# Longer store rows, smaller column slabs and one merged weight load at the end of an attention and soft-MoE kernel

## The chip, the cores and the metric

The kernel runs on one core of one Trainium2 chip. The metric is device time in microseconds (us), median of several executions.

Five engines work side by side: TensorE (PE in the profile, PEld for its weight loads), VectorE (DVE), ScalarE (ACT), GpSimd (POOL) and SyncE (SP). Sixteen DMA engines move data between the main memory (HBM) and the on-chip memory. In this kernel GpSimd issues nearly all loads, because they cast fp32 to bf16 on the way, and SyncE issues the stores (and two early loads). The profile shows the two kinds as queue q0 (software_dynamic) and q1 (hardware_dynamic).

## The reference, cut to what matters

```python
# q, k, v: (8 batches, 8 heads, 576, 64) fp32; windowed attention, first 4 heads plain, last 4 dilated
attn_out = _attn_ref(q, k, v)
x = attn_out.transpose(0, 2, 1, 3).reshape(4608, 512)      # tokens x model width
logits = x @ phi                                            # (4608, 32): 8 experts x 4 slots
d = softmax(logits, axis=0)                                 # over the tokens
slot_input = (d.T @ x).reshape(8, 4, 512)
for e in range(8):                                          # w1: (8, 512, 1024), w2: (8, 1024, 512)
    slot_out[e] = np.maximum(slot_input[e] @ w1[e], 0.0) @ w2[e]
c = softmax(logits, axis=1)                                 # over the slots
return c @ slot_out                                         # (4608, 512) fp32
```

No output token can be made before the last token has been read (softmax over the tokens) and all experts are through, so the 9.4 MB of output can only be stored at the end. The reads are 61.9 MB, 33.6 MB of them expert weights.

## The kernel before

A small scheduler places operations on the engines in an order worked out when the kernel is built, and adds the semaphore waits. The attention runs first; the weights stream in between and behind its inputs on the same queue. The end of the kernel is arranged so that loads and stores join: the second weights of the last experts (w2) are loaded in column slabs. The slab of the first 256 output columns comes first, its results are finished and stored for some tokens, and meanwhile the slab of the other 256 columns arrives. The loads in question:

```python
wq += [w1_piece(e, 2 if e == 0 else 0) for e in range(8)]
wq += [w2_piece(e) for e in range(5)] + [w2_piece(5, 0, 4), w2_piece(5, 4, 4)]   # full rows: 16 KB each in HBM, 8 KB for the halves of 5
for s in range(2):                                                               # two column slabs: rows of 1 KB in HBM
    wq += [w2_slab(6, s), w2_slab(7, s, 0, 4), w2_slab(7, s, 4, 2),
           w2_slab(7, s, 6, 1), w2_slab(7, s, 7, 1)]
```

The second expert layer: columns 0 to 511 at once for experts 0 to 5, then by slab (x = 1, 2) for 6 and 7; an add joins the two parts:

```python
l2((0, 1, 2, 3), 0, 0, 512)
l2((4,), 0, 0, 512)
for y in range(2):
    l2((5,), 0, 0, 512, range(4 * y, 4 * y + 4), [b_w5h[y]])
# ... SOx, SOy: the sums of experts 0 to 5 leave PSUM
for x in (1, 2):
    l2((6,), x, 256 * x - 256, 256, bufs=[b_w2[6][x - 1]])
    for y, cs in enumerate((range(4), range(4, 6), range(6, 7), range(7, 8))):
        l2((7,), x, 256 * x - 256, 256, cs, [b_w2h[y][x - 1]])
    op(DVE, lambda x=x: dve.tensor_tensor( ... AluOp.add) ... name=f"SO{x - 1}")
```

The output: nine groups of 512 tokens, four tiles of 128 tokens in each. A tile is one matmul, then an eviction (scaled copy) on ScalarE or VectorE in turn. The first two and a half groups are stored by column halves (ten stores of 256 KB, rows of 1 KB), half a group as one of 512 KB, the other six in full (stores of 1 MB, rows of 8 KB):

```python
for G, x in halves:                        # 2.5 groups, columns 0 to 255
    for j in (x, x + 1):
        out_tile(G, j, 0, 256, ...)
    store(G, 0, 256, ..., x, 2)
# ... the same for columns 256 to 511
for G, x in [(2, 2)] + [(G, x) for G in range(3, 9) for x in (0, 2)]:
    for j in (x, x + 1):
        out_tile(G, j, 0, 512, T2 + 10 + G + .1 * x)
    if G < NA:
        store(G, 0, 512, T2 + 10 + G + .1 * x + .1, x, 2)
    elif x:
        store(G, 0, 512, T2 + 10 + G + .3)
```

The softmax here doesn't subtract the row's maximum and nothing guards it: scores larger than these inputs give would overflow.

## Time and profile before

| | before |
|---|---|
| time, median (lowest to highest) | 177.54 us (177.39 to 177.60), 3 runs |
| span of the profiled run | 175.6 us |
| busy share: TensorE, VectorE, ScalarE | 73%, 68%, 60% |
| HBM read and written | 61.9 and 9.4 MB, 406 GB/s over the span |
| last weight bytes arrive | 151.38 us |
| first store bytes flow | 149.45 us |
| last store bytes flow | 174.81 us |

The last three rows are from the packet records of the trace. The lines of the profile that carry the reading stand in the prediction below. In the lists of stretches the last two columns are the mean busy share of the 16 DMA engines and the GB/s that they moved. A share can exceed 1, since packets overlap. Loads are counted by the bytes that they write, which is half of what they read.

### The profile page before, as it was taken

The numbers are of one execution on the slowest core, as the hardware profiler recorded it, in microseconds if no ns is written. First come the engines' busy times: TensorE is split into PE (matmuls) and PEld (weight loads), VectorE is DVE, ScalarE is ACT, GpSimd is POOL, SyncE is SP. The second block draws the span as 40 slices with busy tenths as digits, with TensorE's granted clock in tenths as the row PEclk, the third lists the DMA queues.
The fourth block names the chain that finished last, engine by engine and source line by source line (L and its number), as shares of the span: only waits on it lengthen the run. The fifth ranks groups of instructions, "written<-read, shape, count | busy, mean of one in ns | idle before, by whom it ended". The sixth has DMA issues, their size and how long they took to land.

```text
span 175.6 us, 4785 instructions
## 1 busy us (share of the span) xinstructions
PE 128.6 (73%) x2102; PEld 87.1 (50%) x2102; DVE 120.2 (68%) x218; ACT 105.2 (60%) x165; POOL 44.8 (25%) x90
## 2 busy tenths in 40 slices
PE   0008767977999999999998988999576748897000
PEld 0005545665777776766767756777343324531000
DVE  6899387968899898998998898349230013499200
ACT  2404664677988988988969959965603013299000
POOL 7659503402523232207500004950000000000000
PEclk9999995589999999999999999999999996999855
DMA  6999999999999999999999999999999999999997
GB/s 187 233 210 215 210 216 210 223 205 210 222 208 213 225 202 215 217 209 214 216 214 211 216 216 216 215 216 216 218 213 205 207 195 188 301 317 414 424 424 313
DMA packets 15700, 41.26 MB, mean 235 GB/s; under 512 B 1728, under 2 KB 8384, under 8 KB 13248
## 3 DMA queue, kind: packets, MB, share of 16 engines
q0 software_dynamic: 11536, 30.41, 88.9%
q1 hardware_dynamic: 4144, 10.55, 15.8%
q8 instruction: 16, 0.26, 0.5%
q14 instruction: 4, 0.03, 0.0%
HBM read 61.93 MB, written 9.44 MB: 406 GB/s over the span
## 4 chain that ended last, share of the span: by engine, by line
DMA 31%; PE 25%; DVE 22%; ACT 7%; POOL 5%; issue 2%; POOLq 0%; DVEq 0%
DMA ar<-in_moe_w_dram 20%; DMA ar<-in_v_dram 11%; PE ps L527 7%; DVE ar L932 6%; ACT ar L566 5%; DVE ar L495 5%; PE ps L588 3%; POOL ar L379 3%; PE ps L534 2%; PE ps L711 2%; DVE ar L501 2%; DVE ar L632 2%; PE ps L544 2%; PE ps L621 2%; DVE ar L452 2%
## 5 line engine op out<-in xcount | busy, mean ns | idle before, releaser
L566 ACT ACTIVATE ar<-ps 128x1152 bf16<-128x1152 f32 (+1 forms) x32 | 37.9, 1185 | 22.7 <-PE ps L551 11.6
L527 PE MATMUL ps<-ar 128*128 128x320 bf16 (+1 forms) x128 | 23.9, 313 | 16.2 <-DVE ar L501 13.8
L495 DVE STREAM_TRANSPOSE ar<-ar 128x576 uint32<-128x576 uint32 x28 | 32.9, 1233 | 0.5 <-DMA ar<-in_v_dram 0.5
L632 DVE TENSOR_TENSOR ar<-ps,fs 96x768 bf16<-96x768 f32 (+1 forms) x32 | 26.3, 823 | 1.1
L594 ACT ACTIVATE ar<-ps 128x768 bf16<-128x768 bf16 x32 | 24.8, 810 | 2.8 <-PE ps L588 2.3
L527 PEld LDWEIGHTS ps<-ar 128*128 128x128 bf16 x128 | 10.9, 102 | 21.5 <-POOL ar L425 13.7
L621 PE MATMUL ps<-ar 128*128 128x65 bf16 x320 | 15.4, 196 | 3.6 <-ACT ar L566 2.0
L588 PE MATMUL ps<-ar 128*128 128x128 bf16 x192 | 16.2, 233 | 0.5 <-DVE ar L632 0.2
L929 ACT ACTIVATE ar<-ps,fs 128x512 f32<-128x512 f32 (+1 forms) x23 | 11.5, 635 | 8.2 <-PE ps L920 8.2
L621 PEld LDWEIGHTS ps<-ar 128*128 128x128 bf16 x320 | 12.3, 98 | 6.8 <-ACT ar L566 2.9
L343 POOL DMA_DIRECT2D ar<-in_k_dram x14 | 7.5, 541 | 31.8 <-DVE ar L495 16.2
L628 DVE RECIPROCAL fs<-ps 96x12 f32<-96x12 f32 (+1 forms) x32 | 6.5, 204 | 12.7 <-PE ps L621 12.4
L501 DVE STREAM_TRANSPOSE ar<-ar 128x576 uint32<-128x576 uint32 x12 | 14.6, 1241 | 0.0
L588 PEld LDWEIGHTS ps<-ar 128*128 128x128 bf16 x192 | 13.1, 120 | 1.9 <-DVE ar L656 1.0
L932 DVE TENSOR_SCALAR ar<-ps,fs 128x512 f32<-128x512 f32 (+1 forms) x23 | 12.7, 626 | 1.2 <-PE ps L920 1.2
L876 PE MATMUL ps<-ar 128*32 128x512 bf16 (+1 forms) x80 | 10.4, 348 | 4.2 <-DMA ar<-in_moe_w_dram 3.5
L920 PE MATMUL ps<-ar 128*128 128x512 bf16 (+1 forms) x46 | 10.6, 360 | 1.3 <-DVE ar L900 1.0
L711 PE MATMUL ps<-ar 128*128 128x288 bf16 x64 | 10.2, 307 | 1.2 <-ACT ar L695 1.2
L341 POOL DMA_DIRECT2D ar<-in_q_dram x16 | 8.8, 548 | 6.1 <-DVE ar L507 6.1
L688 ACT ACTIVATE ar<-ps 128x576 bf16<-128x576 bf16 x16 | 9.5, 648 | 1.2 <-PE ps L672 0.8
L691 ACT ACTIVATE ar<-ps 128x1024 bf16<-128x1024 bf16 x8 | 8.2, 1030 | 2.9 <-PE ps L678 2.9
L507 DVE STREAM_TRANSPOSE ar<-ar 128x160 uint32<-128x160 uint32 (+1 forms) x32 | 9.6, 413 | 0.0
(78 smaller groups left out, 189.6 us busy)
## 6 DMA issues: line engine op xcount, KB each, us to landing
ar<-in_moe_w_dram POOLq DMA_DIRECT2D x12, 1024.0 KB, 25.0
out_dram<-ar SPq DMA_DIRECT2D x6, 1024.0 KB, 8.6
ar<-in_k_dram POOLq DMA_DIRECT2D x16, 288.0 KB, 13.5
ar<-in_q_dram POOLq DMA_DIRECT2D x16, 288.0 KB, 15.6
ar<-in_v_dram POOLq DMA_DIRECT2D x16, 288.0 KB, 14.3
ar<-in_moe_w_dram POOLq DMA_DIRECT2D x5, 512.0 KB, 31.7
out_dram<-ar SPq DMA_DIRECT2D x10, 256.0 KB, 3.5
ar<-in_moe_w_dram SPq DMA_DIRECT2D x1, 1024.0 KB, 5.0
```

The source lines that it names most:

```text
L495: return dve.transpose(au(o_kqv[kq] + 2304 * j + 36 * x, [[1, 18], [36, 16], [576, 2]]), au(src + 64 * 18 * x, [[32, 18], [1, 32]]))
L501: return dve.transpose(au(dst, [[1, 18], [18, 32]]), au(src, [[32, 18], [1, 32]]))
L527: pe.matmul(pf(h, 0, [[1, W]]), a(o_id, [[1, 128]]), a(msk, [[1, W]]), start=True, stop=False)
L566: eo = op(ACT, lambda P=P, W=W: act.activation(a(P, [[W, 4], [1, W]]), AP(ps, 0, [[4096, 128], [512, 4], [1, W]]), ACTF.Exp, scale=SCALE), ...
L588: last = pe.transpose(pb(bank.idx, bb * 256 + par * 32, [[64, 4], [1, 32]]), src, a(o_id, [[1, 128]]))
L594: op(ACT, lambda t=t, bank=bank: act.activation(a(o_vb[vs] + 3 * t * VBK, [[66, 12], [2, 32], [1, 2]]), pb(bank.idx, 0, [[64, 12], [1, 32] ...
L621: last = pe.matmul(pf(bank.idx + x, 65 * t, [[1, 65]]), w, a(VB + t * VBK + 66 * h, [[1, 65]]), start=True, stop=True)
L632: op(DVE, lambda hp=hp, bank=bank: dve.tensor_tensor(a(ox + 128 * hp, [[64, 2], [256, NT], [1, 64]], 0, rows), pf(bank.idx, 0, [[512, 2], ...
L711: last = pe.matmul(pf(bank.idx, 0, [[1, 288]]), a(o_phis + 128 * c, [[1, 128]]), a(o_xt[xt] + 576 * c + 288 * g, [[1, 288]]), start=(c == ...
L920: op(PE, lambda: pe.matmul(pf(bank.idx, 0, [[1, cw]]), a(o_et + 512 * G + j, [[4, 128]]), a(o_so + c0, [[1, cw]]), start=True, stop=True), ...
L929: op(ACT, lambda: act.activation(dst, src(), ACTF.Copy, scale=sca), actt(cw, .1), prio + .1, reads=[bank, b_rinv], writes=wr, name=f"OE{G} ...
L932: op(DVE, lambda: dve.tensor_scalar(dst, src(), sca, None, op0=AluOp.mult), dvet(cw, True) + .08, prio + .1, reads=[bank, b_rinv], writes= ...
```

## The change

Three things. The column slabs become smaller: the first half of expert 6's hidden rows is loaded in full rows, so the two column slabs together hold 3 MB instead of 4. Expert 5 comes in one transfer. And the last 2048 tokens become two groups of eight tiles, each stored in one transfer of 2 MB with rows of 16 KB. The row sums (the denominators of the second softmax) must be grouped like the output, so they are cut anew. Intent: loads with longer rows, stores with longer rows, and first stores that do not dry up before the second columns are ready. Core of the diff:

```diff
+RS_AT = {13: ((0, 3), (3, 1), (4, 1))}
+RSP = 16
@@
-        if i in (9, 13):
-            row_sums(0 if i == 9 else 3, 3 if i == 9 else 6, 15 * PERIOD)
+        if i in RS_AT:
+            for g, n in RS_AT[i]:
+                row_sums(g, n, RSP * PERIOD + 16)
@@
-    wq += [w2_piece(e) for e in range(5)] + [w2_piece(5, 0, 4), w2_piece(5, 4, 4)]
+    wq += [w2_piece(e) for e in range(6)] + [w2_piece(6, 0, 4)]
     for s in range(2):
-        wq += [w2_slab(6, s), w2_slab(7, s, 0, 4), w2_slab(7, s, 4, 2),
+        wq += [w2_slab(6, s, 4, 4), w2_slab(7, s, 0, 4), w2_slab(7, s, 4, 2),
                w2_slab(7, s, 6, 1), w2_slab(7, s, 7, 1)]
@@
+    GROUPS = [(0, 4), (512, 4), (1024, 4), (1536, 8), (2560, 8), (3584, 8)]
@@
-    for y in range(2):
-        l2((5,), 0, 0, 512, range(4 * y, 4 * y + 4), [b_w5h[y]])
+    l2((5,), 0, 0, 512)
+    l2((6,), 0, 0, 512, range(4), [b_w6h])
@@
-        l2((6,), x, 256 * x - 256, 256, bufs=[b_w2[6][x - 1]])
+        l2((6,), x, 256 * x - 256, 256, range(4, 8), [b_w2[6][x - 1]])
@@
-        op(PE, lambda: pe.matmul(pf(bank.idx, 0, [[1, cw]]), a(o_et + 512 * G + j, [[4, 128]]),
+        op(PE, lambda: pe.matmul(pf(bank.idx, 0, [[1, cw]]), a(o_et + t0 + j, [[n, 128]]),
@@
-    for G, x in [(2, 2)] + [(G, x) for G in range(3, 9) for x in (0, 2)]:
...
+    for G, js in [(2, (2, 3))] + [(G, range(8)) for G in range(3, 6)]:
+        for j in js:
+            out_tile(G, j, 0, 512, T2 + 10 + G + .1 * j)
+            if j == js[-1] or G == 3 and j == 3:
+                n = 4 if G == 3 else len(js)
+                store(G, 0, 512, T2 + 10 + G + .1 * j + .05, j + 1 - n, n)
```

This is an excerpt; cuts are marked by @@ and dots. The first group of eight is still stored in two halves of 1 MB.

More of the change, by code (lines that the diff above doesn't have):

```diff
@@ L310, in bass_dilated_sliding_attn__then__soft_moe_slots_kernel @@
     b_sx = Buf("sx")
-    b_w5h = [Buf(f"w5h{x}") for x in range(2)]
+    b_w6h = Buf("w6h")
     b_w2h = [[Buf(f"w2h{x}{s}") for s in range(2)] for x in range(4)]
@@ L374, in fn @@
                 moe_w2[e].rearrange("(p c) f -> p (c f)", c=8)[:, c0 * DM:(c0 + n) * DM])
-        return (fn, n << 18, f"w2_{e}{c0}", b_w2[e] if e < 5 else [b_w5h[c0 // 4]])
+        return (fn, n << 18, f"w2_{e}{c0}", b_w2[e] if e < 6 else [b_w6h])
     def w2_slab(e, s, c0=0, n=8):
@@ L381, in fn @@
                 moe_w2[e].rearrange("(p c) f -> p c f", c=8)[:, c0:c0 + n, 256 * s:256 * s + 256])
-        return (fn, n << 17, f"w2s_{e}{s}{c0}", [b_w2[e][s] if n == 8 else b_w2h[(0, 4, 6, 7).index(c0)][s]])
+        return (fn, n << 17, f"w2s_{e}{s}{c0}", [b_w2[e][s] if e == 6 else b_w2h[(0, 4, 6, 7).index(c0)][s]])
     wq += [w1_piece(e, 2 if e == 0 else 0) for e in range(8)]
-    wq += [w2_piece(e) for e in range(5)] + [w2_piece(5, 0, 4), w2_piece(5, 4, 4)]
+    wq += [w2_piece(e) for e in range(6)] + [w2_piece(6, 0, 4)]
     for s in range(2):
-        wq += [w2_slab(6, s), w2_slab(7, s, 0, 4), w2_slab(7, s, 4, 2),
+        wq += [w2_slab(6, s, 4, 4), w2_slab(7, s, 0, 4), w2_slab(7, s, 4, 2),
                w2_slab(7, s, 6, 1), w2_slab(7, s, 7, 1)]
@@ L765, in half, with rcol, row_sums @@
            rmw=[b_sid] if b < 7 else [], writes=[b_sdb] if b == 7 else [], name=f"SD{b}")
-    def row_sums(g0, g1, prio):
-        n = (g1 - g0) // 3
-        bank = Bank(f"rs{g0}", n)
+    GROUPS = [(0, 4), (512, 4), (1024, 4), (1536, 8), (2560, 8), (3584, 8)]
+    def rcol(G):
+        return o_rinv + GROUPS[G][0] // 128
+    def row_sums(g0, n, prio):
+        t0, nj = GROUPS[g0]
+        w = 32 * nj * n
+        bank = Bank(f"rs{g0}")
         def fn():
             last = None
-            for m in range(n):
-                for qd in range(4):
-                    last = pe.matmul(pf(bank.idx + m, 0, [[1, 384]], 32 * qd, 32), a(o_rm, [[1, 32]]),
-                                     a(o_et + 512 * (g0 + 3 * m) + 128 * qd, [[512, 3], [1, 4], [4, 32]]),
-                                     start=True, stop=True)
-            return last
-        op(PE, fn, pet(4 * n, 384), prio, reads=[b_et, b_rm], writes=[bank], name=f"RS{g0}")
-        op(DVE, lambda: dve.transpose(af(o_rt, [[384, n], [1, 384]]), pf(bank.idx, 0, [[512, n], [1, 384]])),
-           .1 + .4 * n, prio + .1, reads=[bank], writes=[b_rt], name=f"RT{g0}")
-        op(DVE, lambda: dve.reciprocal(f(o_rinv + 4 * g0, [[1, 12 * n]]), af(o_rt, [[32, 12 * n]])),
+            for qd in range(4):
+                last = pe.matmul(pf(bank.idx, 0, [[1, w]], 32 * qd, 32), a(o_rm, [[1, 32]]),
+                                 a(o_et + t0 + 32 * nj * qd, [[128 * nj, n], [1, nj], [nj, 32]]),
+                                 start=True, stop=True)
+            return last
+        op(PE, fn, pet(4, w), prio, reads=[b_et, b_rm], writes=[bank], name=f"RS{g0}")
+        op(DVE, lambda: dve.transpose(af(o_rt, [[1, w]]), pf(bank.idx, 0, [[1, w]])),
+           .1 + w / 960, prio + .1, reads=[bank], writes=[b_rt], name=f"RT{g0}")
+        op(DVE, lambda: dve.reciprocal(f(rcol(g0), [[1, w // 32]]), af(o_rt, [[32, w // 32]])),
            .2, prio + .2, reads=[b_rt], writes=[b_rinv], name=f"RR{g0}")
@@ L828, in bass_dilated_sliding_attn__then__soft_moe_slots_kernel @@
        reads=[bank], writes=[b_sit], name="sid")
-    row_sums(6, 9, T1 + 4)
+    row_sums(5, 1, T1 + 4)
     for x in range(2):
@@ L878, in fn @@
                                      a(w2off(e) + DM * c + col, [[1, n]]),
-                                     start=(c == 0 and (g == 0 or x > 0)),
-                                     stop=(c == 7 and (x > 0 or e in (2, 3, 4, 5))))
+                                     start=(c == 0 and g == 0 or x > 0 and c == (4 if e == 6 else 0)),
+                                     stop=(c == (3 if e == 6 and x == 0 else 7) and (x > 0 or e in (3, 4, 5, 6))))
             return last
@@ L907, in bass_dilated_sliding_attn__then__soft_moe_slots_kernel, with over @@
     NA = 2.5
-    b_og = [[[Buf(f"og{G}{j}{s}") for s in range(2)] for j in range(4)] for G in range(9)]
+    b_og = [[[Buf(f"og{G}{j}{s}") for s in range(2)] for j in range(n)] for G, (_, n) in enumerate(GROUPS)]
     store_ops = []
-    l1_bufs = b_w1 + [x for y in b_w2[:1] for x in y]
     ne = [0]
     def ostg(G):
-        return o_w1 + 4096 * G if G < 8 else o_w2
+        return o_w1 + 8 * GROUPS[G][0]
+    def over(G):
+        t0, n = GROUPS[G]
+        e = range(t0 // 512, t0 // 512 + n // 4)
+        return [x for y in e for x in ([b_w1[y]] if y < 8 else b_w2[0])]
     def out_tile(G, j, c0, cw, prio):
         bank = Bank(f"o{G}{j}{c0}")
-        t = 4 * G + j
+        t0, n = GROUPS[G]
         rd = [b_so[s] for s in range(2) if c0 < 256 * (s + 1) and c0 + cw > 256 * s]
-        op(PE, lambda: pe.matmul(pf(bank.idx, 0, [[1, cw]]), a(o_et + 512 * G + j, [[4, 128]]),
+        op(PE, lambda: pe.matmul(pf(bank.idx, 0, [[1, cw]]), a(o_et + t0 + j, [[n, 128]]),
                                  a(o_so + c0, [[1, cw]]), start=True, stop=True),
@@ L924, in out_tile @@
         src = lambda: pf(bank.idx, 0, [[1, cw]])
-        wr = [b_og[G][j][s] for s in range(2) if c0 < 256 * (s + 1) and c0 + cw > 256 * s]
-        wr = wr + ([b_w1[G]] if G < 8 else b_w2[0])
-        sca = f(o_rinv + t, [[1, 1]])
+        wr = [b_og[G][j][s] for s in range(2) if c0 < 256 * (s + 1) and c0 + cw > 256 * s] + over(G)
+        sca = f(rcol(G) + j, [[1, 1]])
         if ne[0] % 2 == 0:
@@ L934, in out_tile, with store @@
         ne[0] += 1
-    def store(G, c0, cw, prio, j0=0, n=4):
+    def store(G, c0, cw, prio, j0, n):
+        t0, nj = GROUPS[G]
         rd = [b_og[G][j][s] for j in range(j0, j0 + n) for s in range(2)
               if c0 < 256 * (s + 1) and c0 + cw > 256 * s]
-        dst = out[512 * G:512 * G + 512, c0:c0 + cw].rearrange("(p j) f -> p j f", j=4)[:, j0:j0 + n, :]
+        dst = out[t0:t0 + 128 * nj, c0:c0 + cw].rearrange("(p j) f -> p j f", j=nj)[:, j0:j0 + n, :]
         src = af(ostg(G) + 2 * (512 * j0 + c0), [[512, n], [1, cw]])
@@ L954, in bass_dilated_sliding_attn__then__soft_moe_slots_kernel @@
         store(G, 256, 256, T2 + 10 + G + .25 * x + .2, x, 2)
-    for G, x in [(2, 2)] + [(G, x) for G in range(3, 9) for x in (0, 2)]:
-        for j in (x, x + 1):
-            out_tile(G, j, 0, 512, T2 + 10 + G + .1 * x)
-        if G < NA:
-            store(G, 0, 512, T2 + 10 + G + .1 * x + .1, x, 2)
-        elif x:
-            store(G, 0, 512, T2 + 10 + G + .3)
+    for G, js in [(2, (2, 3))] + [(G, range(8)) for G in range(3, 6)]:
[4 more added lines that the diff above has]
+                store(G, 0, 512, T2 + 10 + G + .1 * j + .05, j + 1 - n, n)
     order = sc.run([4, 5, 6, 7], [0, 1, 2, 3], last_ex[0])
```

## The prediction

> **What bounds the kernel now.** I read the page first: the busy table, then the slices, then the chain of waits. No engine is full (TensorE 73%, VectorE 68%), but the DMA row of the slices is at nine tenths from the second slice to the last but one.
>
> ```profile
> DMA  6999999999999999999999999999999999999997
> GB/s 187 233 210 215 210 216 210 223 205 210 222 208 213 225 202 215 217 209 214 216 214 211 216 216 216 215 216 216 218 213 205 207 195 188 301 317 414 424 424 313
> q0 software_dynamic: 11536, 30.41, 88.9%
> q1 hardware_dynamic: 4144, 10.55, 15.8%
> HBM read 61.93 MB, written 9.44 MB: 406 GB/s over the span
> ```
>
> The rate of some 213 GB/s counts bytes written: the loads read fp32 and write bf16, so from HBM they run at twice that. At the right end, where only stores run, it is 414 to 424. The kernel is 71 MB of traffic; time can be saved only by moving the same bytes faster or by closing holes in the transfers. Of the chain of waits in order of time I read the end:
>
> ```profile
> 116.14 35.60 DMA ar<-in_moe_w_dram
> 151.73 0.04 issue
> 151.78 0.30 PE ps L876
> 152.07 0.02 issue
> 152.10 0.44 DVE ar L900
> 152.54 0.05 issue
> 152.58 0.42 PE ps L920 x2
> 153.01 0.02 issue
> 153.03 8.63 DVE ar L932 x15
> 161.66 0.66 DVEq L1013
> 162.32 1.32 DVE ar L932 x2
> ```
>
> The last weight slab lands at 151.7, one matmul and one add finish the slot outputs, then the output tiles are evicted. The line of evictions looks like the bound of the end, but it ends at 163.6 and the span at 175.6: the last 11 us are the store queue draining. So next I asked for busy time and transfer rates in stretches that I chose from the half-microsecond rates:
>
> ```profile
> core 0: us, PE busy (x) PEld busy (x) DVE busy (x) ACT busy (x) POOL busy (x), PEclk, DMA share, GB/s
> 134.00:139.00 5.00, 4.08 (x50) 2.42 (x51) 0.36 (x2) 0.32 (x1) 0.00 (x0) 1.00 1.04 204
> 144.00:148.00 4.00, 3.18 (x19) 1.55 (x18) 0.46 (x2) 0.25 (x1) 0.00 (x0) 0.66 1.45 196
> 149.30:151.40 2.10, 1.86 (x14) 0.99 (x12) 0.79 (x3) 0.51 (x2) 0.00 (x0) 1.00 1.20 264
> 151.40:153.30 1.90, 1.30 (x10) 0.91 (x10) 0.70 (x2) 0.38 (x2) 0.00 (x0) 1.00 1.04 364
> 153.30:154.60 1.30, 1.30 (x10) 0.76 (x7) 1.30 (x4) 1.30 (x5) 0.00 (x0) 1.00 0.57 200
> 158.50:174.80 16.30, 2.83 (x10) 0.63 (x9) 5.14 (x8) 3.86 (x7) 0.00 (x0) 0.72 1.00 413
> ```
>
> Read the last two columns. Full-row loads write 204 to 215, column slabs 196 (their rows are 1 KB in HBM), slabs with stores among them 264, stores of 1 KB rows 364, stores of 8 KB rows 413. One stretch is a hole: from 153.3 to 154.6 the DMA share is 0.57 and the rate 200 where 360 is possible. There the five stores of the first output columns run out before those of the second columns are issued.
>
> **What the Trainium skill says.** "DMA: Bandwidth & Descriptors", section Where 436 GB/s comes from, puts the ceiling at 435 GB/s; the 8 KB rows here are at 413 to 424, so at most some 4% is left in them. The same page, Why small descriptors are slow, gives a fixed cost of about 3 beats of 32 B per packet: 3 on 256 for an 8 KB row, 3 on 512 for 16 KB, so an estimate of 0.6% saved. The trace agrees in direction: in its packet records a store row of 1 KB takes 46 ns in the median, one of 4 KB 166 ns, one of 8 KB 314 ns. The section Issuing engines are not separate DMA queues says that transfers of all issuers share the same 16 DMA engines; the trace agrees, since in 149.3 to 151.4 the rate of 264 is a mixture and not 196 plus 364. Nothing there says what a slab of another width does to the hole; that I work out.
>
> **The change part by part.**
>
> *Slabs of 3 MB.* The column slabs were all of experts 6 and 7 (2.1 MB of HBM for each half of the columns, 4.2 in all). Now the first half of expert 6's hidden rows is loaded in full rows ahead of them, and each slab has 1.57 MB. Bytes stay the same. First effect: 0.52 MB as written goes at 204 to 215 instead of 196: 0.524/0.196 = 2.67 us against 0.524/0.21 = 2.50, so 0.2 us saved on the bound resource.
>
> Second effect: the order in time. The packet records, counted back from the last load, have half of the slab bytes moved at 144.8, the last at 151.4; the first add (L900) follows at 146.8, the first store is issued at 148.5, and its bytes flow from 149.35. So first bytes of a store come 4.55 us after the first slab's bytes. The second slab alone takes 1.05/0.196 = 5.35 us before the change and 0.786/0.196 = 4.0 us after. Before, the five first stores (1.31 MB, 3.6 us at 364) start under the second slab and dry up at 153.3 to 154.6. After, the first slab's bytes are through at 139.5 + 0.524/0.21 + 4.0 = 146.0, the loads at 150.0 to 150.4 and the first stores flow from 150.5: behind the loads and not among them. They last until 150.5 + 3.6 = 154.1 to 154.5. The second stores need, as before, the last landing (150.5), the add (0.3 after it) and 2.45 us from the add to flowing bytes (152.1 to 154.55 now): 153.3 at the best.
>
> But this chain gets a new neighbour. The output tiles of the first columns, which ran from 147.3 to 150.1, shift by some 1.1 us, and VectorE takes its instructions in order: its five evictions would end near 151.2, and only then comes the second add. TensorE likewise does its ten output matmuls first, to some 150.0, and then twelve slab matmuls of 131 ns (eight took 1.05 us), 1.6 us, to 151.6 or so. So the second stores flow at 153.7 to 154.1, still about when the first run out. The hole at 153.3 (1.3 us at 0.57 of full rate, some 0.55 us lost) closes, and a new one of 0 to 0.5 us can open between the end of the loads and the first stores at 150.0 to 150.5. Net: I take 0.2 us saved of a possible 0.55.
>
> *Expert 5 in one transfer.* Two transfers of 512 KB become one of 1 MB with rows twice as long. The number of issues on GpSimd stays the same (expert 6 gains one full-row transfer), and these were all issued by 117. TensorE waits for expert 5 until 141.0 and has 3 us until the slab; the extra four matmuls of expert 6 fit there. 0 us.
>
> *16 KB rows.* Output groups 5 to 8 (2048 tokens, 4.19 MB) become two groups of eight tiles: four stores of 1 MB become two of 2 MB. They take 4.19/0.413 = 10.15 us now. From the overhead estimate above 0.06 us is saved; from the packet medians (the step from 4 to 8 KB costs 36 ns per KB, so 16 KB would take 610 ns against twice 314) up to 16 x 18 ns = 0.29 us on each engine. I take 0.1. A store of eight tiles must wait for eight evictions: 8 x 0.33 = 2.6 us (26 tiles took 8.6 us), against 5 us that a 2 MB store takes. The first of the two is complete near 161 and its turn on the queue comes near 164, the second 163.7 and 169. No starvation.
>
> *Row sums.* The sums over slots are cut anew: three rounds of twelve columns become four (twelve, eight, eight, eight), so one VectorE transpose and reciprocal more, some 0.6 us (0.57 and 0.23 for the old size), and all of them later. The order listing shows them between 110 and 130 us, where VectorE idles afterwards; the load queue runs until 151. 0 us. The weights of the output matmuls are read with a step of eight columns instead of four; no trace here shows a price for it, and TensorE is free then.
>
> Sum: 0.2 + 0.2 + 0.1 = 0.5 us out of 177.5. I discount it a little for the rivals: 177.1.
>
> **The rivals.** (1) *The hole only moves.* If the loads end at 150.0 and stores begin at 150.5, and TensorE delays the second add, the lost 0.55 us comes back in two pieces, and only slab rows and long rows remain: 0.2 to 0.3 us, 177.3. For it: VectorE and TensorE both have the first columns' output in front of the second add. Against it: the slab arrives earlier than before by the contention that it no longer has. (2) *Half of the engines set the end.* A share of 0.57 in the hole could mean that half of the 16 DMA engines are drained while the others still work; these slow ones have no idle time, and closing the hole for the fast half gains nothing. Then 177.3 to 177.5. The views don't separate engines. (3) *Evictions or issue as the bound of the end.* They end at 163.6 with 11 us of stores behind them; they would have to be 1.5 times slower to matter. Ruled out, as near as can be. (4) *All adds up*: hole closed in full and 0.29 us from the rows: 176.6. (5) *Larger transfers end unevenly*, an engine's last packet being 0.6 us long instead of 0.3: up to 0.3 us lost, 177.8 together with (1).
>
> **Range and chances.** From (4) to (5), 176.5 to 177.8, around 177.1. The 2% line lies at 3.55 us. The only thing that the change touches at the bound is 10 us of stores and 7 us of slabs; to gain 2% would need 20% of these, above the ceiling, and to lose as much a stall that no view hints at. So within 2% is near certain; I leave 2% for faster and 2% for slower.
>
> **What would show it.** In the changed kernel's rates: about 210 until some 142 and 196 from there; the last weight landing near 150.4 instead of 151.7; no stretch with share 0.57 near 154, perhaps a dip near 150.4; the stretch of the large stores at 415 to 425 instead of 413; the DMA end near 174.2. Wrong would be: the first stores still mixed with the loads; a gap of over 1 us ahead of the second columns' stores, with VectorE's add (L900 now) after 152.5; a rate below 413 with 16 KB rows; or any shift before 130 us, which would mean that the row sums or the new schedule disturbed the loads.

## The result, and the profile after

The changed kernel takes 176.98 us (176.90 to 177.15, 6 runs) against 177.57 us (177.34 to 177.67, 6 runs) of before. The ratio is 0.997, with a 95% interval of 0.9957 to 0.9982. Ratios here are the mean time of one kernel's runs over that of the other's of the same rounds, so they are not quite the ratio of the medians. It is a gain of 0.5 us, well inside the 2% that counts as the same, and close to the 177.1 predicted. The span of the profiled run fell from 175.6 to 175.2.

The chain of waits of the changed kernel, its end in order of time (start, length, what):

```profile
115.33 36.21 DMA ar<-in_moe_w_dram
151.54 0.04 issue
151.58 0.30 PE ps L885
...
151.90 0.44 DVE ar L909
...
152.84 8.63 DVE ar L945 x15
```

The last landing is at 151.54 where it was at 151.73, and the second add (line 909 now) runs at 151.90 where it ran at 152.10: 0.2 us earlier. The prediction had the last landing near 150.5. So the end came out about right, but not by the path foretold. Busy time and transfer rates of the changed kernel in stretches:

```profile
core 0: us, PE busy (x) PEld busy (x) DVE busy (x) ACT busy (x) POOL busy (x), PEclk, DMA share, GB/s
148.00:149.00 1.00, 0.71 (x7) 0.71 (x8) 0.49 (x2) 0.37 (x1) 0.00 (x0) 1.00 1.23 163
149.00:150.00 1.00, 0.97 (x10) 0.63 (x7) 1.00 (x4) 1.00 (x4) 0.00 (x0) 1.00 0.77 103
151.40:153.30 1.90, 1.27 (x11) 0.94 (x10) 0.89 (x3) 0.57 (x2) 0.00 (x0) 1.00 1.06 361
153.30:154.60 1.30, 1.30 (x9) 0.74 (x8) 1.30 (x5) 1.30 (x5) 0.00 (x0) 1.00 0.95 329
```

The hole at 153.3 to 154.6 is gone (329 GB/s where it was 200). In its place there is a hole ahead of the stores: from 149 to 150 the loads move 103 GB/s, half of the 194 to 196 of a slab, though no store is flowing yet (the first store packet starts at 150.16). Before the change the loads fell off at the same time (171 GB/s from 148.5 to 149.0, 132 in the next half microsecond), and I had read the 264 GB/s of the stretch that follows as loads and stores competing on the same engines. The next list shows another split: half of the engines have no loads left, and the other half still load.

That is seen in the trace one level below the profile's views. Each transfer ends with sixteen semaphore increments; I read them as one for each of the 16 DMA engines, and the runs with moved rows below bear that out. Here are those of the last weight load, sorted, in us from the start of the span:

```
before:  148.77 149.04 149.10 149.31 149.33 149.48 149.62 150.29 | 151.16 151.38 151.51 151.53 151.60 151.67 151.72 151.73
changed: 148.69 148.87 148.91 148.93 149.03 149.17 149.21 149.77 | 151.05 151.26 151.34 151.36 151.38 151.42 151.43 151.54
```

Eight engines are through by 149.8 (150.3 before), the other eight end 1.3 to 2.9 us later. The last matmul needs all sixteen. The first stores are queued on all sixteen as well, so a late engine does its share of them after its last load: the eight late completions of the first store come 0.7 us after those of the last load. Before the change the five first stores end at 154.62, after it at 154.39, though their bytes start to flow 0.7 us later than before: their end follows the late engines and not the start of the stores.

From there the two kernels run alike for a while. The gain of 0.23 us at 154.4 is 0.25 at 164.6, where the last 4.19 MB begin. Those take 9.99 us before and 9.82 us with 16 KB rows. 0.25 + 0.17 = 0.42 us, which is what the profiled runs differ by (177.41 and 176.99). (All from the packet records.)

So two theories stood against each other. **Theory P**, the prediction's: the 16 engines are one pool, and a hole in it costs time wherever it is. **Theory S** (its second rival): the eight late engines set the load end and the end of the first stores; idle time of the early ones is free.

### The profile page after: what moved, and what is told of

It reads as the page before. It is cut to its first block, busy times and chain, and to the rows that moved or that the text cites. A ratio compares the mean times of both kernels' runs of the same rounds, so it can differ in the third digit from the quotient of the medians.

```text
span 175.2 us, 4785 instructions
## 1 busy us (share of the span) xinstructions
PE 127.4 (73%) x2102; PEld 86.0 (49%) x2102; DVE 120.7 (69%) x220; ACT 105.1 (60%) x165; POOL 44.5 (25%) x90
## 4 chain that ended last, share of the span: by engine, by line
DMA 33%; DVE 24%; PE 22%; ACT 7%; POOL 5%; issue 3%; POOLq 0%; DVEq 0%
DMA ar<-in_moe_w_dram 21%; DMA ar<-in_v_dram 12%; PE ps L529 6%; DVE ar L497 6%; DVE ar L945 6%; ACT ar L568 4%; POOL ar L381 3%; DVE ar L503 3%; PE ps L590 2%; PE ps L713 2%; PE ps L536 2%; DVE ar L634 2%; PE ps L623 2%; PE ps L546 2%; DVE ar L454 2%
## 5 line engine op out<-in xcount | busy, mean ns | idle before, releaser
L529 PE MATMUL ps<-ar 128*128 128x320 bf16 (+1 forms) x128 | 23.2, 306 | 16.1 <-DVE ar L503 13.8
L529 PEld LDWEIGHTS ps<-ar 128*128 128x128 bf16 x128 | 10.8, 100 | 20.9 <-POOL ar L427 13.7
L623 PEld LDWEIGHTS ps<-ar 128*128 128x128 bf16 x320 | 12.1, 98 | 6.7 <-ACT ar L568 2.9
L590 PEld LDWEIGHTS ps<-ar 128*128 128x128 bf16 x192 | 12.7, 118 | 3.7 <-DVE ar L634 2.3
## 6 DMA issues: line engine op xcount, KB each, us to landing
ar<-in_q_dram POOLq DMA_DIRECT2D x16, 288.0 KB, 16.2
```

Of the source, the lines that this page charges most:

```text
L529: pe.matmul(pf(h, 0, [[1, W]]), a(o_id, [[1, 128]]), a(msk, [[1, W]]), start=True, stop=False)
L590: last = pe.transpose(pb(bank.idx, bb * 256 + par * 32, [[64, 4], [1, 32]]), src, a(o_id, [[1, 128]]))
L623: last = pe.matmul(pf(bank.idx + x, 65 * t, [[1, 65]]), w, a(VB + t * VBK + 66 * h, [[1, 65]]), start=True, stop=True)
```

## The experiments

Twelve kernels ran, all with correct results. Where a run has a bracket, it is the 95% interval of its ratio to the kernel before.

### Long store rows alone

Edit: the changed kernel with the loads and the second layer of before.

```diff
-    wq += [w2_piece(e) for e in range(6)] + [w2_piece(6, 0, 4)]
+    wq += [w2_piece(e) for e in range(5)] + [w2_piece(5, 0, 4), w2_piece(5, 4, 4)]
-        wq += [w2_slab(6, s, 4, 4), ...
+        wq += [w2_slab(6, s), ...
```

> The changed kernel with the loads of before (column slabs of 4.2 MB, expert 5 in two transfers): only the 16 KB store rows and the row sums regrouped for them. Theory P (the prediction: the 16 DMA engines are one pool, the hole at 153 us has a price): 0.1 us faster than before, the hole at 153.3 to 154.6 stays with a DMA share near 0.57. Theory S (two halves: 8 engines finish the loads 2.8 us after the other 8 and set the end, the hole of the early 8 has no price): the hole stays too; the last 4.19 MB of stores take 9.8 us instead of 10.0, so 0.15 to 0.25 us faster than before in time. In both the loads end where they ended before, 151.4 us.

Measured: 177.37 us against 177.49 of before, ratio 0.9995 [0.9982, 1.0008]. The last 4.19 MB took 9.83 us (9.99 before), much as in the whole change (9.82); a 16 KB row takes 615 ns in the median, two of 8 KB took 2 x 314. The hole stays, as the stretch of this run shows (columns as above; the last two are DMA share and GB/s):

```profile
153.20:154.70 1.50, 1.31 (x11) 1.10 (x10) 1.49 (x4) 1.50 (x5) 0.00 (x0) 1.00 0.55 194
```

What follows: the long rows bring 0.16 us where they are stored. The whole time shows only 0.1 us, within noise; in the profiled run the last landing was at 151.91, 0.18 us later than in the profile of before, which cancels the gain. Both theories had the loads end where they ended before, so that is a miss. Most of it is spread and not a slower pool: the mean of the sixteen completions is 150.51, against 150.45 before. Why the last engine was later I can't say; the regrouped row sums are in this run too.

### Slabs and merged load alone

Edit: the changed kernel with nine output groups of four tiles; row sums and store loop follow.

```diff
-    GROUPS = [(0, 4), (512, 4), (1024, 4), (1536, 8), (2560, 8), (3584, 8)]
+    GROUPS = [(512 * g, 4) for g in range(9)]
```

> The changed kernel with the stores of before (nine output groups of four tiles, 8 KB rows): only the slabs of 3.1 MB and expert 5 in one transfer. Theory P: 0.4 us faster than before, of which 0.2 from the closed hole. Theory S: only what the longer load rows bring to the late 8 engines counts, 0.2 to 0.25 us; loads end at 151.2, the first five stores at 154.4. Together with the run of long rows alone the two must add up to the whole change, about 0.55 us.

Measured: 177.18 us against 177.49, ratio 0.9980 [0.9968, 0.9992]. The first five stores end at 154.40 (154.62 before), the last 4.19 MB take 9.98 us. The last landing is at 151.53. The hole is closed here too, as its stretch in this run shows:

```profile
153.30:154.60 1.30, 1.11 (x8) 0.68 (x8) 1.30 (x5) 1.30 (x5) 0.00 (x0) 1.00 0.91 314
```

What follows: 0.2 us in the profile and 0.3 in the medians. The profile gives the load end 0.2 us earlier and nothing for the closed hole, as theory S has it; the interval of the times (0.14 to 0.57 us) alone would not tell the two apart. The two parts add up to 0.25% (0.05 + 0.20) against 0.3% of the whole.

### Expert 5 in one transfer alone

Edit: the kernel before with one load for two.

```diff
-    wq += [w2_piece(e) for e in range(5)] + [w2_piece(5, 0, 4), w2_piece(5, 4, 4)]
+    wq += [w2_piece(e) for e in range(6)]
```

> The kernel before, with the second weights of expert 5 in one transfer and nothing else changed. Both theories: no change, within 0.1 us of before; the matmuls on it start at about the same 141 us, since they wait for its last part anyway.

Measured: 177.45 us against 177.63, ratio 0.9997 [0.9984, 1.0010]. Load end and first stores are those of before (151.43 and 154.63). No effect, as expected.

### Slabs of 2 MB

Edit: all of expert 6 in full rows, slabs of expert 7 alone (the add then covers one expert's rows only).

```diff
-    wq += [w2_piece(e) for e in range(6)] + [w2_piece(6, 0, 4)]
+    wq += [w2_piece(e) for e in range(7)]
-        wq += [w2_slab(6, s, 4, 4), w2_slab(7, s, 0, 4), w2_slab(7, s, 4, 2),
+        wq += [w2_slab(7, s, 0, 4), w2_slab(7, s, 4, 2),
```

> The changed kernel with slabs of 2.1 MB (all of expert 6 in full rows, slabs of expert 7 alone). Full rows gain another 0.15 us of loads, but the first slab ends later. Theory P, taken further: first stores flow about 1.2 us after the loads end on all engines, so 0.7 us slower than the changed kernel. Theory S: the late 8 engines have no work from their load end near 151.1 until the first stores flow near 151.4 and no stores done before; their first stores end at 151.4 + 3.6 = 155.0 instead of 154.4: 0.5 us slower than the changed kernel, about as fast as before the change.

Measured: 179.07 us (178.09 to 180.18, 6 runs) against 177.49, ratio 1.0086 [1.0059, 1.0113]. Slower as both theories said, but by 2.1 us against the changed kernel and not by 0.5 or 0.7. The stretches of this run show why:

```profile
core 0: us, PE busy (x) PEld busy (x) DVE busy (x) ACT busy (x) POOL busy (x), PEclk, DMA share, GB/s
146.00:148.50 2.50, 2.50 (x12) 1.20 (x12) 0.00 (x0) 0.00 (x0) 0.00 (x0) 0.50 1.44 193
...
151.00:152.40 1.40, 1.40 (x15) 1.13 (x13) 1.40 (x4) 1.40 (x5) 0.00 (x0) 1.00 0.00 0
152.40:156.30 3.90, 2.97 (x20) 2.08 (x19) 3.36 (x9) 2.81 (x9) 0.00 (x0) 1.00 1.01 337
```

From 151.0 to 152.4 nothing moves at all: the loads end at 150.96 and the first stores flow at 152.43. I had put that start at 151.4. As I read the trace, the extra microsecond comes from TensorE: the whole of expert 6 is computed just before the slab, and the granted clock was 0.50 from 146.0 to 148.5, so its matmuls and those of the first slab fill 145.85 to 149.1 and the slab's sum came late (no run tried it without the low clock). What follows: the slab must be long enough that the first stores are in the queue before the late engines run dry. This run has the earliest load end of all (150.96) and the longest time, so the load end alone is not the bound. The 3 MB of the change stand on the right side of that edge, with the first store bytes at 150.16 and the late engines loading until 151.2.

### Moving rows of a load from one group of engines to the other

If eight engines set the end, giving them less to do must help, and giving one of them more must hurt, at the same total of bytes. A load of 112 partitions has seven rows for each of the 16 engines; a load of 8 partitions should use eight engines only, which the completions below bear out. Edit, in the changed kernel:

```diff
-    wq += [w2_piece(e) for e in range(6)] + [w2_piece(6, 0, 4)]
+    wq += [w2_piece(e) for e in range(4)]
+    wq += [w2_rows(4, *r) for r in                      # tag, first partition, partitions, first element, elements
+           (("a", 0, 112), ("b", 112, 8), ("c", 120, 8, 0, 256), ("d", 120, 8, 256, 3840))]
+    wq += [w2_piece(5), w2_piece(6, 0, 4)]
```

> The changed kernel with the 1 MB load of expert 4 cut: 112 partitions (7 rows on each of 16 engines), and the last 16 partitions in transfers of 8 partitions each, which should run on 8 engines only (a tiny one of 8 x 256 elements lies between them in case the choice of the 8 alternates). So 8 engines get up to two rows of 16 KB more than the other 8. Theory P: total bytes count, no change, or 0.1 slower for the added transfers. Theory S: the spread between the first and the last of the 16 completions of a late load, 2.8 us, changes by about 1.2 us, down if the 8 that get more rows are the early ones (then loads end 0.6 us earlier and the time falls by some 0.5 us), up if they are the late ones (0.6 us slower). If the 8 engines chosen are a mixture, the spread shows a third group and the time stays.

Measured: 177.55 us, 0.57 more than the changed kernel's median. The sixteen completions of the last load:

```
changed: 148.69 148.87 148.91 148.93 149.03 149.17 149.21 149.77 151.05 151.26 151.34 151.36 151.38 151.42 151.43 151.54
shifted: 148.37 148.47 149.47 149.70 149.81 149.84 149.87 150.36 150.45 150.48 150.52 150.54 150.72 150.76 152.07 152.10
```

The third case of the expectation: a mixture. Two engines end at 148.4 (early, a row less), two at 152.1 (late, a row more), twelve between, since six early ones got more and six late ones less. But the time did not stay, as I had written for this case: it rose by 0.57 us, as much as the last completion (0.56), although fourteen of sixteen engines were done by 150.8. The mean of the sixteen is where it was (150.22 against 150.21), so the pool as a whole was no slower. What follows: theory P is out, and the end follows the very last engine, not the mean of the eight late ones.

### Trying to move the set

Two runs put tiny transfers ahead, to move the set of eight on by two or by fourteen of sixteen places. Edit: the list of pieces only.

```diff
+(("a", 0, 112), ("t", 112, 2, 0, 256), ("b", 112, 8, 256, 3840), ("u", 120, 8, 0, 256), ("c", 120, 8, 256, 3840), ("v", 114, 6, 0, 256))
```

```diff
+(("a", 0, 112), ("t", 112, 8, 0, 256), ("u", 112, 4, 256, 256), ("v", 116, 2, 256, 256), ("b", 112, 8, 512, 3584),
+ ("w", 120, 8, 0, 256), ("c", 120, 8, 256, 3840), ("x", 118, 2, 256, 256))
```

> As the shift run, but a tiny transfer of 2 partitions ahead, so that the 8 engines of the extra rows are two further on, if a small transfer takes engines from where the last small one stopped. In the shift run 6 of the 8 chosen were early engines and 2 late ones; those 2 ended at 152.07, the rest by 150.8. If the set moves in the wrong direction there are 4 late ones in it (4 completions at 152.1, time as in the shift run, 177.5); in the right direction none is (last load completion near 150.8 instead of 151.5, 0.5 us faster than the changed kernel); if the set does not move, the shift run is repeated: 177.5, 2 completions at 152.1. Theory P: no change of time in any case, 177.0 to 177.1.

> As the shift run, with tiny transfers of 8, 4 and 2 partitions ahead, which would move the set of 8 by 14 of 16, that is 2 back. One of this run and the run with 2 ahead should have no late engine among the 8 (theory S: last load completion near 150.8, first five stores done by 154.0, 0.5 us faster than the changed kernel, 176.5), unless the set is fixed (then 177.5 again). Theory P: 177.0 to 177.2.

Measured: 177.63 us (4 runs) and 177.65 us (5 runs); two engines end last in both, at 152.08 and 152.17, and at 152.01 and 152.18. The set doesn't move. A third run used groups of 6, 6 and 4 partitions, which need not be the same engines:

```diff
+(("a", 0, 112), ("b", 112, 6), ("c", 118, 6), ("d", 124, 4))
```

> The load of expert 4 cut into 112, 6, 6 and 4 partitions. If small transfers always start at the first engine, engines 0 to 3 get three rows more than 6 of the others and engines 4 and 5 two. If the two late engines of the shift run were the last two of its eight, no late engine gets more: last load completion near 150.3 (late engines have a row less, 0.6 us, than in the changed kernel) and 0.5 us faster; the early ones with 3 rows end near 150.0. If the two were the first ones, they end 1.2 us later than in the changed kernel, 152.7, and the time is 1.1 us longer. Theory P: no change.

Measured: 177.74 us (4 runs). One engine ends last, at 152.35; the next at 151.58, then all by 151.09. So of the first six engines of the small transfers one is a late one. Neither of my two cases fits in full (150.3 or 152.7).

### Four groups of four

Edit, in the same place:

```diff
+(("a", 0, 112), ("b", 112, 4), ("c", 116, 4), ("d", 120, 4), ("e", 124, 4))
```

> The load of expert 4 cut into 112 partitions and four transfers of 4, in the changed kernel. The runs before showed that the set of engines of a small transfer is fixed: of the first 8 two are late ones, of the first 6 one. Now the first 4 engines get 11 rows, the other 12 get 7. Theory S: if none of the first 4 is a late one, the last load completion comes at 150.7 to 150.9 (late engines have one row of 0.6 us less than the 151.5 of the changed kernel), the early ones with 11 rows end near 150.5, the first five stores near 154.0, and the time is 176.4 to 176.6, 0.4 to 0.5 us less than the changed kernel. If one of the first 4 is a late one, it ends at 151.4 + 1.9 = 153.3 and the time is 178.8. Theory P: 177.0 to 177.2 in either case.

Measured: 177.16 us, ratio 0.9982 [0.9968, 0.9995]. Completions: four at 148.27 to 148.85, eleven at 150.51 to 151.11, and one at 151.78. So the first four are early engines, as hoped, and the late ones gained some 0.5 us; one engine ends after all of them, and the time went with it: 0.2 us more than the changed kernel, though the two intervals overlap. The time is in neither of my two ranges for theory S, for the straggler was not foreseen; it lies in the range given for theory P (177.0 to 177.2), so this run by itself does not speak against P.

The straggler is not a late engine. The early ones are not alike: one is at 149.77 in the changed kernel, the other seven by 149.21. In the last load before the cut of this run one early engine is 1.06 us behind the first. If it is one of the four that took rows, it has four rows more than an early engine that took none; the loads in full rows ahead of the cut took 4.87 us for 8 rows of each engine, 0.61 a row. So an estimate is 1.06 + 2.43 = 3.49 us behind the first; measured 3.51 (151.78 - 148.27). The late ones, 0.6 us earlier than the changed kernel's, would be done by 151.0.

The same with the load of expert 3 or of expert 5 cut in place of expert 4's:

```diff
-    wq += [w2_piece(e) for e in range(4)] + [w2_rows(4, *r) for r in FOURS] + [w2_piece(5)] + [w2_piece(6, 0, 4)]
+    wq += [w2_piece(e) for e in range(3)] + [w2_rows(3, *r) for r in FOURS] + [w2_piece(4), w2_piece(5)] + [w2_piece(6, 0, 4)]
```

```diff
+    wq += [w2_piece(e) for e in range(5)] + [w2_rows(5, *r) for r in FOURS] + [w2_piece(6, 0, 4)]
```

FOURS stands for the five pieces above.

> The run of four small transfers again, with the load of expert 3 cut instead of expert 4's. In that run 15 of the 16 engines had finished by 151.1, one ended at 151.8, and the time followed that one (177.16). Over the runs with long store rows the time follows the last of the 16 completions one for one: 151.54 gives 176.98, 152.10 gives 177.55, 152.35 gives 177.74. Theory S: time = 176.98 + (last completion - 151.54), within 0.15; if the single straggler is gone, the last is 151.1 and the time 176.55. If it comes with the number of small transfers, it stays at 151.8 and 177.2.

> The same with the load of expert 5 cut, which is later in the queue. The same expectation: time = 176.98 + (last of the 16 completions of the last load - 151.54), within 0.15; 176.55 without the straggler, 177.2 with it. TensorE waits for the pieces of expert 5 near 141 and has slack, so no other effect.

Measured: 177.43 us (177.25 to 177.83) and 177.34 us (177.17 to 177.57), last completions 151.73 and 151.84. The straggler is there in both, and the same estimate gives it: 1.25 + 2.43 = 3.68 us behind the first engine for expert 3 (measured 3.69), 1.18 + 2.43 = 3.61 for expert 5 (3.60). The rule foretold 177.17 and 177.28: the second holds, the first is missed by 0.26 in the median (its profiled run took 177.25). No kernel of this series beats the changed one. So only three of the four engines that took rows had room for three more. The trace doesn't number the engines, so the straggler is identified by these sums and not by a run of its own.

### What makes eight engines late

The spread of the sixteen completions is not there from the start. In the changed kernel it is 0.7 us for a load that ends at 22.5 us, 1.7 at 80 us and 2.8 from 86 us on. In the sorted completions one engine after the other falls back by about 1.1 us: by 82 us eight have done so once, at the end eight have done so twice. The steps come as often as the packets of the queue that carries instructions, here from the list of DMA queues of the changed kernel (packets, MB, share of the 16 engines' span):

```profile
q8 instruction: 16, 0.26, 0.5%
```

Sixteen packets of 16 KB, the first at 23.6, the last at 139.4, eight of them before 80, each 0.89 to 0.98 us long. The Trainium skill, "Runtime: NRT & Kernel Launch", section Instruction fetch mechanics, says that an engine's instructions are refilled in blocks of 16 KiB, 256 instructions, by a DMA queue of its own, and that the cost is mostly hidden. TensorE has 2102 matmuls and 2102 weight loads here, 16.4 such blocks: the trace agrees with the count. Whether they make the engines late is a matter for an experiment. Edit, in the changed kernel: 256 tiny matmuls in TensorE's first 13 us, when it has nothing to do; nothing reads their result.

```diff
+        def idle_fn(bank=bank):
+            for _ in range(256):
+                last = pe.matmul(pf(bank.idx, 0, [[1, 8]], 0, 32), a(o_vb[0], [[1, 32]]),
+                                 a(o_vb[0], [[1, 8]]), start=True, stop=True)
+            return last
+        op(PE, idle_fn, 9.0, -200.0, reads=b_vb[0], writes=[bank], name="idle")
```

> What makes eight engines late: the trace of the changed kernel has 16 instruction packets of 16 KB of 0.89 to 0.98 us, one after the other at the pace at which TensorE consumes instructions, and the gap between the completions of early and late engines opens by 1.1 us at each on one engine, twice on each of eight. Here 256 tiny matmuls whose result is not used (512 instructions with their weight loads, 32 KB) run in TensorE's idle first 13 us; the order of all other instructions is the same. If theory S and this cause hold, there are 18 instruction packets, two engines get a third one, the last completion comes 0.8 to 1.1 us later than 151.54, and the time is 177.8 to 178.1, though the added traffic is 32 KB (0.08 us over 16 engines). If the skew has another cause, the time stays at 177.0 to 177.1 and the spread at 2.8.

Measured: 178.06 us (177.81 to 178.10), 1.08 more than the changed kernel. The instruction queue of this run:

```profile
q8 instruction: 18, 0.29, 0.6%
```

The completions of the last load:

```
changed:        148.69 148.87 148.91 148.93 149.03 149.17 149.21 149.77 151.05 151.26 151.34 151.36 151.38 151.42 151.43 151.54
with 32 KB more: 148.98 149.00 149.14 149.15 149.17 149.30 149.47 149.71 150.97 150.99 151.01 151.11 151.44 151.46 152.32 152.52
```

Fourteen engines are where they were, within 0.4 us; two are one step later, at 152.3 and 152.5. The steps are seen where they begin: the added packets are at 9.4 and 16.2 us, and by the load that ends at 12.1 us one engine has fallen 0.7 us behind the others, by 19.1 us a second one. The stretches of this run, over 149 to 151, show most engines out of work:

```profile
core 0: us, PE busy (x) PEld busy (x) DVE busy (x) ACT busy (x) POOL busy (x), PEclk, DMA share, GB/s
149.00:150.00 1.00, 0.65 (x6) 0.65 (x7) 0.50 (x2) 0.31 (x1) 0.00 (x0) 1.00 0.77 102
150.00:151.00 1.00, 1.00 (x10) 0.68 (x8) 1.00 (x4) 1.00 (x4) 0.00 (x0) 1.00 0.61 81
```

What follows: 512 more TensorE instructions, run when TensorE was idle, cost 1 us at the far end of the kernel, because each block of 16 KB falls on one DMA engine of a kernel that is bound by DMA. That is shown for the two added blocks. That the sixteen blocks of the changed kernel fall twice on each of eight engines and make up the spread is read from the timing of the steps, which are of about that size.

### The runs with the changed kernel's stores and slabs, in one table

Last of the sixteen completions of the last load, time of the same profiled run, and median:

| run | last completion | profiled run | median |
|---|---|---|---|
| changed kernel | 151.54 | 176.99 | 176.98 |
| four groups of 4, expert 3 | 151.73 | 177.25 | 177.43 |
| four groups of 4, expert 4 | 151.78 | 177.28 | 177.16 |
| four groups of 4, expert 5 | 151.84 | 177.34 | 177.34 |
| 8 and 8 | 152.10 | 177.55 | 177.55 |
| 8 and 8, tiny transfer of 2 ahead | 152.17 | 177.64 | 177.63 |
| 8 and 8, tiny transfers of 8, 4 and 2 ahead | 152.18 | 177.62 | 177.65 |
| 6, 6 and 4 | 152.35 | 177.82 | 177.74 |
| 32 KB more instructions | 152.52 | 178.07 | 178.06 |

Over these nine, the profiled time is 176.99 + (last completion - 151.54) within 0.1 us. In them the late engines delay the first slab by as much as the second, so alone they would not separate the end of the loads from the start of the stores. The run of long rows alone does: its first stores flow a microsecond earlier (149.21), and it fits as well, 151.91 giving 177.36 against 177.37 measured. With 0.17 us added for 8 KB rows, the rule also gives the three others: 177.35 for the kernel before (151.73; measured 177.41), 177.15 for slabs and merged load alone (151.53; 177.20), 177.40 for expert 5 alone (151.78; 177.45). Only the slabs of 2 MB are outside it; there the first stores come after the end of the loads on every engine.

## Why the prediction was right or wrong

The time, 177.1, and its range held. Step by step:

- **DMA is the bound.** Right. In no run but that with slabs of 2 MB did the computing of an engine show in the time.
- **Longer load rows, 0.2 us.** Right: load end 151.38 to 151.23, last landing 151.73 to 151.54. The last landing scatters (151.91 and 151.78 in two other runs with the loads of before); the mean of the sixteen completions less: 150.38 to 150.51 in three runs with the loads of before, 150.21 and 150.23 in two with those of the change.
- **The loads at 150.0 to 150.4, the last landing at 150.5.** Wrong by 1 us. The failed step is the one that called the stretch of 264 GB/s "a mixture" in which loads lose to stores, and let the loads end earlier once no stores flow among them. The loads fell to 103 GB/s with no store flowing, because eight engines had none left. The sixteen completions would have shown it in the trace of before, in which the spread was 2.97 us. As a mean over the engines the forecast was good (150.21); but the kernel waits for the last of them, 1.3 us later.
- **First stores at 150.5, last of them done at 154.1 to 154.5, the second columns just in time.** The values came out (150.16, 154.39, no hole at 154), the first for the reason given, the others because the late engines carry them.
- **The closed hole, 0.2 us net.** Wrong: the profile leaves nothing for it. Only early engines had been idle. The hole moved ahead of the stores, as the first rival said, and it was free in either place, as the second rival said. Rival 2 held, with its time (177.3 to 177.5) too high, partly since it left the long rows out.
- **16 KB rows, 0.1 us.** Under-sized: 0.17 us in the stores themselves, midway between the estimate from the overhead in the skill (0.06) and the most that the packet medians allowed (0.29).
- **Expert 5, row sums, eight tiles to a store: 0.** Expert 5 measured alone, ratio 0.9997. The second columns and the stores of eight tiles never starved. The row sums were not tried alone.

- **The signs it named.** One of its signs of being wrong came: the first stores still overlap the loads, from 150.16 to 151.23 (149.45 to 151.38 before). The others did not: the second add is at 151.90; the large stores, in the prediction's stretch from 158.5 to their end at 174.41, run at 418 GB/s (413 before; the view gives 408 up to 174.8, but from 174.41 nothing moves); the loads ahead of 130 us land where they did (116.65 against 116.58).

That the sum of 0.5 came out is partly luck: the missing 0.2 us of the hole was in part made up by the rows. The medians moved by 0.59 us, the profiled runs by 0.42; single runs of the kernel before lie 0.33 us apart.

## What to carry to other kernels

When a kernel is bound by DMA, the mean share of the 16 engines hides which of them is last; compare the sixteen completions of one late transfer before giving a hole a price, since a transfer is only done with its last engine. Idle time on engines that are ahead costs nothing, and a hole may be closed or moved without gain. A long unrolled instruction stream is DMA traffic too, and it falls on some of the engines only: here 32 KB of it cost 1 us of 177.

## What the Trainium skill lacked or had wrong

- "Runtime: NRT & Kernel Launch", Instruction fetch mechanics, calls the cost of a 16 KiB block mostly hidden. Here each block took 0.89 to 0.98 us of one DMA engine, and two more blocks made this DMA-bound kernel 1.08 us slower (178.06 against 176.98). The page doesn't say that each block occupies a single DMA engine, which other transfers then wait for; completions show eight of sixteen behind by 1.3 to 2.9 us.
- "DMA: Bandwidth & Descriptors", Latency and other measured facts, names engines 7 and 15 as usually slower, with SWDGE ring contention as a guess. Here it is eight engines, and the steps by which they fall behind come with the instruction packets. The trace does not number the engines, so whether 7 and 15 are among them stays open.
- The same page, Why a DMA increments its semaphore by 16 and not by 1, has small SWDGE transfers use consecutive engines from a round-robin cursor, with an exception on trn2. In the runs with tiny transfers ahead the set didn't move: two engines ended last at 152.1 to 152.2 without them, with 2 partitions and with 14 partitions ahead. That fits a fixed start and not a cursor. The exception, whose examples are of 100 and 127 partitions, would give a fixed start if it holds for small transfers too; the page doesn't say for which it holds.
- No page gives the gain from 8 to 16 KB rows of a store; here 615 ns against 2 x 314 ns a row, 9.82 us against 9.99 us for 4.19 MB.
